# Max products in two pairs of PSUM banks, two exp banks in place of three: one core, attention with an MLP behind it

## The chip, the cores and the metric

One core of a Trainium2 chip runs the whole program. The metric is device time in microseconds, the median of several executions. TensorE (PE) multiplies matrices into PSUM, which has eight banks of 128 partitions x 512 fp32 here; VectorE (DVE) and ScalarE (ACT) read PSUM; GpSimd (POOL) works on SBUF alone; SyncE (SP) issues the DMAs.

## The reference, cut to what matters

```python
mod = (silu(c) @ w_mod).reshape(1, 6, 1, 512)          # sa, ca, ga, sb, cb, gb
h = layernorm(x) * (1 + ca) + sa                       # x: 2048 x 512
q = (h @ wq).reshape(2048, 32, 16); k = h @ wk; v = h @ wv   # 32 heads, one k and v of 16
p = softmax(einsum("hqd,kd->hqk", q, k) / 4)
x = x + ga * (einsum("hqk,kd->qhd", p, v).reshape(2048, 512) @ wo)
h = layernorm(x) * (1 + cb) + sb
x = x + gb * (gelu(h @ w1 + b1) @ w2 + b2)             # w1: 512 x 1376
```

All heads share one k and one v. Everything is fp32 in and out; products that need the precision are made from a high and a low part of each operand (three products in place of one).

## The kernel before, in words

**Units.** The 2048 queries are cut into eight blocks of 256, the 32 heads into eight groups of four: 64 units. The transposed queries of a unit lie in a tile `qst`, the keys in `ks`. Both have two row halves (s = 0: partitions 0 to 63, s = 1: 64 to 127), so that two products with 64 rows each can run side by side in TensorE's array, one per half. The functions take s as an argument.

**Two passes over the scores.** Softmax needs the largest score of each query. `Max.step` (L502) makes one *max product* (L509: 128 queries of one head against 512 keys, one PSUM bank `m`), and VectorE takes the maxima of its rows (L514, 128x512 to 128x1). A unit has 32 of them, the program 2048. When a unit is complete, `put_max` (L530) takes the last maxima, transposes them and sends them by DMA into extra rows of `qst`, from where they take part in the second pass. `sexp` (L576) makes one *exp product* (L589: 128 keys against 512 queries, bank `e0`, `e1` or `e2`, or `x`), already less the maximum, and ScalarE writes its exponential to SBUF (L590). There are 2048 of these too. `pv` (L592) multiplies the exponentials with v: 16 products of L601 per block, which use all 128 rows, into bank `v`.

**PSUM before.** Three banks for maxima (tag `m`), three for exps (`e0`, `e1`, `e2`), one for accumulation (`v`), one (`x`) for everything else: late q projections, the output projection, the MLP. Where no such job holds `x`, the plain half cycles put their last max product there.

**The order is written by hand.** All five engines run their instructions in the order in which the Python code issues them; a counter `clock` stands for time, and `later(n, fn)` puts a step n ticks ahead. The main loop goes over the 64 units and, in each, over pairs of key steps X = K and Y = K + 1. One turn of it makes eight exp products and, by the leads of `lead`, usually eight max products (for units some six half cycles ahead), in two *half cycles*, each closed by a P.V block (`end_step`, L1295).

- If a *batch* is at hand (`take`: up to six products with 512 columns, or twelve with 256, of another job: w1, w2, the output projection `wops`, late q projections, transposes), each of its products is split by rows: `half(one, 0)` runs in the first half cycle, `half(one, 1)` in the second. These *fills* occupy one row half; the four max products and three exps are placed on the other, alternately, and the fourth exp follows the fills. Exp banks are 0, 1, 2, 0.
- Without a batch (`plain`, L1323), two exps and two max products go to each row half.

`issue` (L1275) merges the lists of the two row halves into one order for TensorE: every entry has a length, and the list whose lengths add up to less is served next. A fill has 0.75 of its length, so that fills are issued a little early.

**What else shares the engines.** VectorE also drains w1's results and the output projection, ScalarE does Square and Tanh of GELU, POOL the rest of GELU and all splitting in the main loop. The last block has no attention beside it (`fast`): its projection and MLP run alone at the end, and take their PSUM banks from a list `spread`.

Of the kernel before, what the change touches and what calls it, by code (L numbers as in the profile page):

```python
# [14 lines left out]
P = 128  # L15
# [33 lines left out]
def adaln_mqa_mlp(  # L49
# [70 lines left out]
    turns = [0]  # L120

    def ebank():
        turns[0] += 1
        return dict(tag=f"e{turns[0] % 3}", bufs=1)
# [145 lines left out]
    def keep_warm(n):  # L270

        for _ in range(n):
            ps = psum.tile([P, BQ], F32, name=f"idle{len(idles)}", tag="m", bufs=3)
            nc.tensor.matmul(ps, wkH[:, 0, :], wkH.rearrange("p k n -> p (k n)"), start=True, stop=True)
            idles.append(ps)
# [84 lines left out]
    def turn1(b, d):  # L360
        ps = psum.tile([P, BQ], F32, name=f"tp{b}_{d}", **ebank())
# [36 lines left out]
    def v_out(b):  # L398
        vt = vts.pop(b)
        pv_ = psum.tile([P, QT, 32], F32, name=f"vps{b}", **ebank())  # L400
# [83 lines left out]
    class Max:  # L484


        def __init__(self):
# [9 lines left out]
            self.mx, self.left, self.done = {}, list(size), 0  # L497
# [4 lines left out]
        def step(self, s, hold=None, **place):  # L502
            u, j, t, kc = self.todo[s].pop(0)
            T = blocks[units[u][0]][1] // P
            if u not in self.mx:
                self.mx[u] = att.tile([P, 4 * T, NKC], F32, name=f"mx{u}", tag="mx", bufs=2)
            m = psum.tile([P, 512], F32, name=f"m{u}_{j}_{t}_{kc}_{s}", **(place or dict(tag="m", bufs=3)))
            rows = slice(64 * s, 64 * s + 64)
            nc.tensor.matmul(m, qsts[u][rows, j, t * P:(t + 1) * P], ks[rows, kc * 512:(kc + 1) * 512],  # L509
                             start=True, stop=True)  # L510
            i = (s * 2 + j) * T + t

            def reduce():
                nc.vector.tensor_reduce(out=self.mx[u][:, i, kc:kc + 1], in_=m, axis=AX.X, op=ALU.max)  # L514
                self.left[u] -= 1
                if self.left[u] == size[u] // 2 and u > 1 and u + 1 < NU:
                    load_q(u + 1)
                if self.left[u] == 0:
                    put_max(u, self.mx.pop(u))

            self.done += 1
            if hold is None:
                reduce()
            else:
                hold.append(reduce)
# [4 lines left out]
    def put_max(u, mx):  # L530
# [31 lines left out]
        def reduce():  # L562
            nc.vector.tensor_reduce(out=mm[:, :4 * T], in_=mx, axis=AX.X, op=ALU.max)
# [123 lines left out]
    def rest(b, fast):  # L687
# [3 lines left out]
        spread = ["m", "e", "m", "e", "m", "e", "v"] if fast else ["x"]  # L691
        turn = [0]

        def bank():
            turn[0] += 1
            tag = spread[turn[0] % len(spread)]
            return ebank() if tag == "e" else dict(tag=tag, bufs=3 if tag == "m" else 1)
# [54 lines left out]
        return rest_steps(b, fast, rp, bank, ons, ready)  # L752
# [27 lines left out]
    def rest_steps(b, fast, rp, bank, ons, ready):  # L780
# [4 lines left out]
        for hf in range(w // HQ):  # L785
# [44 lines left out]
            for t in range(2):  # L830
                ps = psum.tile([P, D], F32, name=f"wops{b}_{hf}_{t}", **bank())
# [49 lines left out]
            if fast:  # L881
                tps = [psum.tile([P, 2, HQ], F32, name=f"tp2_{b}_{hf}_{dp}", **bank()) for dp in range(KD // 2)]
# [9 lines left out]
            else:  # L892
                for dp in range(KD // 2):
                    ps = psum.tile([P, 2, HQ], F32, name=f"tp2_{b}_{hf}_{dp}", **bank())
# [43 lines left out]
            if fast:  # L938
                group = {f: psum.tile([P, HQ], F32, name=f"w1ps{b}_{hf}_{f}", **bank()) for f in range(GROUP)}
# [9 lines left out]
            for f in range(GROUP if fast else 0, NF):  # L949
# [3 lines left out]
                ps = psum.tile([P, HQ], F32, name=f"w1ps{b}_{hf}_{f}", **bank())  # L953
# [22 lines left out]
            for t in range(2):  # L976
                sl = slice(t * P, (t + 1) * P)
                for cols in (slice(0, D), ):
                    place = dict(tag="m", bufs=3) if b == len(blocks) - 2 and t else bank()
                    ps = psum.tile([P, D], F32, name=f"w2ps{b}_{hf}_{t}_{cols.start}", **place)  # L980
# [156 lines left out]
    def chunk(n):  # L1137
        for _ in range(n):
            mp.step(mp.done % 2)
# [93 lines left out]
    def last_h(t):  # L1233
        if t == QT - 1:
# [10 lines left out]
            "wq 1": one(prep_wq, 1), "wq 2": one(prep_wq, 2), "wq 3": one(prep_wq, 3)}  # L1245
    for n, *names in SLOTS:
# [22 lines left out]
    while mp.done < lead[0]:  # L1269
        chunk(1)  # L1270
# [14 lines left out]
    def mixture(a, b):  # L1285

        out = []
        while a or b:
            if a:
                out.append(a.pop(0))  # L1290
            if b:
                out.append(b.pop(0))
        return out

# [9 lines left out]
    for u in range(NU):  # L1304
        for K in range(0, steps[u], 2):
            goal = lead[u] + (lead[u + 1] - lead[u]) * (K + 2) / steps[u]
            goal = min(goal, first[u + QBUFS] if u + QBUFS < NU else first[NU])
            n = max(0, 2 * round((goal - mp.done) / 2))

            def maxes(s, n, first_=1.0, held=None):  # L1310
                return [(1.0 if i else first_, lambda i=i: mp.step(s, held if i == 2 else None)) if mp.has(s) else (0.0, lambda: None)
                        for i in range(n)]

            def exps(s, which):
                return [(1.0, lambda K=K, j=j, bank=bank: sexp(u, K, j, s, bank)) for K, j, bank in which]
# [114 lines left out]
```

## Time and profile before

| | |
|---|---|
| three runs, median | 1601.61 us (1600.05 to 1605.82) |
| profiled execution | 1599.49 us |
| its span, first to last instruction | 1597.6 us |
| mean granted TensorE clock | 0.996 |
| maxima L514 on VectorE | 2048, 1271.4 us busy |
| exponentials L590 on ScalarE | 2048, 1069.4 us busy |
| first P.V block after the span's start | 83.4 us |

A group of the profile names the line, the engine, the operation and the tiles (`mx<-m`: tile mx is written, tile m is read). PE rows are products, PEld rows the loading of their stationary operand; a product of one row half appears as 64 rows. A wait is written as engine and line that waited, then what it waited for. In the timeline, neighbouring instructions of one group are merged, with their count behind an x.

### The profile page before, as it was taken

How to read it: one execution, taken by the hardware profiler on the slowest of the kernel's cores; microseconds unless marked ns; L12 is line 12 of the kernel's file. 1: busy time of each engine (PE TensorE's matmuls, PEld its weight loads, DVE VectorE, ACT ScalarE, POOL GpSimd, SP SyncE). 2: the span in 40 equal slices, each digit the busy share in tenths (PEclk: the TensorE clock that was granted, in tenths of full speed). 3: DMA queues.
4: the chain of work that ended last, by engine and by line, in shares of the span. 5: the costliest groups of instructions: out<-in, count | busy, mean ns of one | idle time of the engine just before them, and what ended most of it. 6: DMA issues, size and time to landing. Idle time of an engine off the chain costs nothing.

```text
span 1597.6 us, 41064 instructions
## 1 busy us (share of the span) xinstructions
PE 1560.3 (98%) x16369; PEld 1006.3 (63%) x16369; DVE 1412.9 (88%) x2473; ACT 1203.0 (75%) x2393; POOL 666.1 (42%) x1176
## 2 busy tenths in 40 slices
PE   5999999999999999999999999999999999999998
PEld 3466665557665676657665676656666576656667
DVE  6899999899999998999989999999999999999715
ACT  5577778778777887778877887778877787778853
POOL 4445344747422571246413462234602474225711
PEclk8999999999999999999999999999999999999999
DMA  7136312313022220303112120213112130122232
GB/s 257 73 109 205 117 68 71 125 32 107 17 63 65 68 68 25 103 17 106 32 44 84 53 85 22 78 42 98 42 35 91 42 98 18 62 72 64 80 132 74
DMA packets 79285, 121.59 MB, mean 76 GB/s; under 512 B 15774, under 2 KB 52382, under 8 KB 78836
## 3 DMA queue, kind: packets, MB, share of 16 engines
q1 hardware_dynamic: 79076, 118.95, 23.2%
q8 instruction: 128, 2.10, 0.6%
q14 instruction: 65, 0.53, 0.1%
q10 hardware_dynamic: 16, 0.00, 0.0%
HBM read 91.13 MB, written 27.27 MB: 74 GB/s over the span
## 4 chain that ended last, share of the span: by engine, by line
PE 90%; DVE 6%; DMA 2%; POOL 1%; SPq 1%; ACT 0%; issue 0%; DVEq 0%; POOLq 0%
PE acc L601 30%; PE m L509 22%; PE e L589 17%; PE w1ps L184 8%; DVE mx L514 5%; PE w2ps L184 4%; PE wops L184 2%; PE qps L184 1%; PE w2ps L178 1%; DMA xt<-in_A_x_dram 1%; PE w1ps L178 1%; PE tp L184 1%; PE kps L160 1%; DMA qst<-dq 1%; DVE st L807 0%; DMA os<-drs 0%
## 5 line engine op out<-in xcount | busy, mean ns | idle before, releaser
L514 DVE TENSOR_REDUCE mx<-m 128x1 f32<-128x512 f32 x2048 | 1271.4, 682 | 107.6 <-PE m L509 81.3
L590 ACT ACTIVATE p<-e 128x512 f32<-128x512 f32 x2048 | 1069.4, 599 | 311.1 <-PE e L589 233.2
L509 PE MATMUL m<-ks,qst 64*128 64x512 f32 x2048 | 823.9, 425 | 17.4 <-DVE mx L514 11.0
L589 PE MATMUL e<-qst,ks 64*128 64x512 f32 x2048 | 739.1, 409 | 2.8 <-ACT p L590 1.5
L601 PE MATMUL acc<-p,va 128*32 128x256 f32 x8192 | 550.5, 386 | 0.6 <-DMA qst<-dq 0.6
L509 PEld LDWEIGHTS m<-ks,qst 64*128 64x128 f32 x2048 | 364.1, 184 | 185.8 <-DVE mx L514 157.0
L589 PEld LDWEIGHTS e<-qst,ks 64*128 64x128 f32 x2048 | 366.6, 185 | 85.2 <-ACT p L590 59.5
L601 PEld LDWEIGHTS acc<-p,va 128*32 128x32 f32 x8192 | 214.9, 109 | 220.6 <-issue 115.7
L184 PE MATMUL w1ps<-h2H,w1t 64*128 64x256 f32 x1232 | 236.3, 288 | 0.0
L558 POOL TENSOR_SCALAR mt<-turned 8x32 f32<-8x32 f32 x256 | 53.2, 208 | 362.4 <-DVE turned L564 350.4
L184 PEld LDWEIGHTS w1ps<-h2H,w1t 64*128 64x128 f32 x1232 | 184.2, 185 | 31.7 <-issue 23.0
L184 PE MATMUL w1ps<-h2L,w1t 64*128 64x256 f32 x616 | 169.4, 275 | 0.0
L184 PE MATMUL w2ps<-w2H,gH 64*128 64x512 f32 x286 | 118.1, 413 | 0.0
L184 PE MATMUL w2ps<-w2L,gH 64*128 64x512 f32 x286 | 117.4, 411 | 0.0
L184 PE MATMUL w2ps<-w2H,gL 64*128 64x512 f32 x286 | 117.4, 410 | 0.0
L184 PEld LDWEIGHTS w1ps<-h2L,w1t 64*128 64x128 f32 x616 | 113.8, 185 | 0.0
L920 POOL TENSOR_SCALAR tt<-tt 128x256 f32<-128x256 f32 x77 | 31.1, 404 | 162.8 <-ACT tt L919 162.8
L744 POOL TENSOR_TENSOR os<-os 128x256 f32<-128x256 f32 x28 | 20.6, 734 | 100.9 <-DMA os<-drs 100.2
L921 POOL TENSOR_TENSOR tt<-tt,z 128x256 f32<-128x256 f32 x77 | 57.1, 741 | 6.4
L135 POOL TENSOR_TENSOR gL<-z,gH 128x256 fp32r<-128x256 f32 x77 | 56.8, 738 | 6.4
L931 POOL TENSOR_TENSOR z<-tt,z 128x256 f32<-128x256 f32 x77 | 56.5, 733 | 6.0
L930 POOL TENSOR_TENSOR tt<-tt,z 128x256 f32<-128x256 f32 x77 | 56.7, 736 | 0.0
(188 smaller groups left out, 1498.2 us busy)
## 6 DMA issues: line engine op xcount, KB each, us to landing
w1t<-dw SPq DMA_DIRECT2D x82, 512.0 KB
qst<-dq SPq DMA_DIRECT2D x128, 64.0 KB
do<-oc SPq DMA_DIRECT2D x64, 128.0 KB
dw<-w1s SPq DMA_DIRECT2D x11, 512.0 KB
xt<-in_A_x_dram SPq DMA_DIRECT2D x4, 1024.0 KB
dq<-qH SPq DMA_DIRECT2D x16, 256.0 KB
dq<-qL SPq DMA_DIRECT2D x16, 256.0 KB
qst<-dq SPq DMA_DIRECT2D x128, 32.0 KB
```

The costliest lines, as they stand in the source:

```text
L135: eng_l.tensor_tensor(out=dst_l, in0=src, in1=raw(dst_h), op=ALU.subtract)
L178: nc.tensor.matmul(ps, a, b_, start=first_, stop=last_)
L184: nc.tensor.matmul(ps, a[rows], b_[rows], start=first_ and s == 0, stop=last_ and s == 1)
L509: nc.tensor.matmul(m, qsts[u][rows, j, t * P:(t + 1) * P], ks[rows, kc * 512:(kc + 1) * 512], start=True, stop=True)
L514: nc.vector.tensor_reduce(out=self.mx[u][:, i, kc:kc + 1], in_=m, axis=AX.X, op=ALU.max)
L558: nc.gpsimd.tensor_scalar(out=mt[:, g:g + 32], in0=turned[g:g + 4 * T, :], scalar1=1.0, scalar2=0.0, op0=ALU.mult, op1=ALU.add)
L589: nc.tensor.matmul(e, ks[rows, kt * P:(kt + 1) * P], rhs, start=True, stop=True)
L590: nc.scalar.activation(ptiles[u, K][:, j, s, :], e, AF.Exp, scale=0.25)
L601: ins = nc.tensor.matmul(accs[u][32 * cidx:32 * cidx + 32, :], va[:, kt, :], rhs, start=kt == 0, stop=kt == NKT - 1)
L921: nc.gpsimd.tensor_tensor(out=tt, in0=tt, in1=z, op=ALU.mult)
L930: nc.gpsimd.tensor_tensor(out=tt, in0=tt, in1=z, op=ALU.mult)
L931: nc.gpsimd.tensor_tensor(out=z, in0=tt, in1=z, op=ALU.add)
```

## The change

It replaces the three `m` banks and one `e` bank by two tiles of two banks each (`pairs`). A pair gets two max products of the same row half in the main loop, of both row halves at the start (`both`); VectorE takes the maxima of both in one instruction, whose output is two columns of `mx`. The number of products is the same. Exps have banks `e0` and `e1`, and `x` in plain half cycles where no job holds it.

The half cycles are ordered anew: in one with a batch the fills' row half begins with an exp, and the other has two max products, an exp, a max product, an exp, a max product, an exp. Plain half cycles have one pair on each row half. The results of the last block and of the start go to `single` banks of the pairs where they went to `m`.

```diff
+    pairs = [psum.tile([P, 2, 512], F32, name=f"m{i}") for i in "ab"]
+    singles = [pair[:, i, :] for pair in pairs for i in range(2)]
+    turns = {"e": 0, "m": 0, "both": 3}
...
+    def eplace(shape, name):
+        turns["e"] += 1
+        i = turns["e"] % turns["both"]
+        if i == 2:
+            return shaped(singles[3], shape)
+        return psum.tile(shape, F32, name=name, tag=f"e{i}", bufs=1)
...
-        def step(self, s, hold=None, **place):
+        def product(self, out, s):
...
-            nc.tensor.matmul(m, qsts[u][rows, j, t * P:(t + 1) * P], ks[rows, kc * 512:(kc + 1) * 512],
+            nc.tensor.matmul(out, qsts[u][rows, j, t * P:(t + 1) * P], ks[rows, kc * 512:(kc + 1) * 512],
                              start=True, stop=True)
...
-                nc.vector.tensor_reduce(out=self.mx[u][:, i, kc:kc + 1], in_=m, axis=AX.X, op=ALU.max)
...
+        def reduce(self, pair, one, two):
+            u, i = one
+            assert two[0] == u and two[1] > i
+            nc.vector.tensor_reduce(out=self.mx[u][:, i:two[1] + 1:two[1] - i], in_=pair, axis=AX.X, op=ALU.max)
+            self.left[u] -= 2
...
+        def both(self):
+
+            pair = self.next_pair()
+            self.reduce(pair, *[self.product(pair[:, s, :], s) for s in range(2)])
+
+        def pair(self, s, hold=None):
...
+            return [(1.0, lambda: ends.append(self.product(pair[:, 0, :], s))), (1.0, last)]
...
-        spread = ["m", "e", "m", "e", "m", "e", "v"] if fast else ["x"]
+        spread = ["m", "e", "m", "e", "m", "m", "v"] if fast else ["x"]
...
     def chunk(n):
-        for _ in range(n):
-            mp.step(mp.done % 2)
+        for _ in range(n // 2):
+            mp.both()
...
+    turns["both"] = 2
     for n, *names in SLOTS:
...
-            n = max(0, 2 * round((goal - mp.done) / 2))
+            n = max(0, round((goal - mp.done) / 4))
...
-            def plain(s, K, t, n, banks):
-
-                a, b_, c_, d = banks
-                one = mixture(exps(s, [(K, 0, a), (K, 1, c_)]), maxes(s, n))
-                other = maxes(t, n)
+            def beside(batch, s, exps, go_on_=None, held=None):
+
+                fills = halves(batch, s) + ([(0.0, go_on_)] if go_on_ else [])
+                ms = [m for i in range(n) for m in mp.pair(1 - s, held if i == 1 else None)]
+                issue([(1.01, exps[0][1])] + fills, ms[:2] + [exps[1]] + ms[2:3] + [exps[2]] + ms[3:] + [exps[3]])
+
+            def plain(K, banks, more):
 
                 soon = any(planned and time <= clock[0] + 2 for time, _, planned in queue)
-                if not holder and not soon and mp.has(t) and n > 1:
-                    other[-1] = 1.0, lambda: mp.step(t, tag="x", bufs=1)
-                issue(one, exps(t, [(K, 0, b_)]) + other + exps(t, [(K, 1, d)]))
+                free = not holder and not soon
+                a, b_, c_, d = more if free else banks
+                one, other = mp.pair(1) if n > 1 else [], mp.pair(0) if n else []
+                issue([(1.01, exp(0, K, 0, a)[1])] + other + [exp(0, K, 1, d)], one + [exp(1, K, 0, b_), exp(1, K, 1, c_)])
...
             if batch:
-                groups = [mixture(maxes(1, n // 2, 0.0), exps(1, [(X, 0, 0), (X, 1, 1), (Y, 0, 2)])),
-                          halves(batch, 0) + exps(0, [(X, 0, 0)])]
-                issue(*(reversed(groups) if batch[0][3] else groups))
+                beside(batch, 0, [exp(0, X, 0, 0), exp(1, X, 0, 1), exp(1, X, 1, 0), exp(1, Y, 0, 1)])
             else:
-                plain(1, X, 0, (n + 2) // 4, (1, 2, 0, 1))
+                plain(X, (0, 1, 0, 1), (0, 1, "x", 0))
...
-                issue(mixture(maxes(0, n // 2, 0.0, reduces), exps(0, [(X, 1, 0), (Y, 0, 1), (Y, 1, 2)])),
-                      halves(batch, 1) + [(0.0, go_on_)] + exps(1, [(Y, 1, 0)]))
+                beside(batch, 1, [exp(1, Y, 1, 1), exp(0, X, 1, 0), exp(0, Y, 0, 1), exp(0, Y, 1, 0)], go_on_, reduces)
                 advance()
             else:
-                plain(1, Y, 0, n // 4, (2, 0, 1, 2))
+                plain(Y, (0, 1, 0, 1), (1, "x", 0, 1))
```

More of the change, by code (lines that the diff above doesn't have):

```diff
@@ new lines, in product, with next_pair @@
+            return u, ((s * 2 + j) * T + t) * NKC + kc
+        def reduce(self, pair, one, two):
[3 more added lines that the diff above has]
+            self.left[u] -= 2
+            if self.left[u] == size[u] // 2 and u > 1 and u + 1 < NU:
+                load_q(u + 1)
+            if self.left[u] == 0:
+                put_max(u, self.mx.pop(u))
+        def next_pair(self):
+            self.turn = 1 - self.turn
+            return pairs[self.turn]
@@ L751, in rest @@
         later(*((4, lambda: norm(0)) if fast else (2, fetch)))
-        return rest_steps(b, fast, rp, bank, ons, ready)
+        return rest_steps(b, fast, rp, place, ons, ready)
     early = {}
@@ L938, in rest_steps @@
             if fast:
-                group = {f: psum.tile([P, HQ], F32, name=f"w1ps{b}_{hf}_{f}", **bank()) for f in range(GROUP)}
+                group = {f: place([P, HQ], f"w1ps{b}_{hf}_{f}") for f in range(GROUP)}
                 for k in range(KD):
@@ L978, in rest_steps @@
                 for cols in (slice(0, D), ):
[L979 to L980 removed]
+                    ps = single([P, D]) if b == len(blocks) - 2 and t else place([P, D], f"w2ps{b}_{hf}_{t}")
                     ops = [(gH[:, f, sl], gL[:, f, sl], w2H[:, f, cols], w2L[:, f, cols]) for f in range(NF)]
@@ L1283, in issue @@
             at[g] += length
[L1285 to L1293, printed above, removed]
     def end_step(u, K):
@@ L1307, in adaln_mqa_mlp, with exp @@
             goal = min(goal, first[u + QBUFS] if u + QBUFS < NU else first[NU])
-            n = max(0, 2 * round((goal - mp.done) / 2))
[L1310 to L1315, printed above, removed]
+            n = max(0, round((goal - mp.done) / 4))
+            def exp(s, K, j, bank):
+                return 1.0, lambda: sexp(u, K, j, s, bank)
             def halves(batch, s):
```

62 lines of the change are left out of this document (32 added, 30 removed).

## Prediction

> **What bounds the kernel now.** I read the page's busy times first, then its chain and groups, then the waits, and last the timeline, half cycle by half cycle.
>
> ```profile
> PE 1560.3 (98%) x16369; PEld 1006.3 (63%) x16369; DVE 1412.9 (88%) x2473; ACT 1203.0 (75%) x2393; POOL 666.1 (42%) x1176
> PE 90%; DVE 6%; DMA 2%; POOL 1%; SPq 1%; ACT 0%; issue 0%; DVEq 0%; POOLq 0%
> L514 DVE TENSOR_REDUCE mx<-m 128x1 f32<-128x512 f32 x2048 | 1271.4, 682 | 107.6 <-PE m L509 81.3
> L590 ACT ACTIVATE p<-e 128x512 f32<-128x512 f32 x2048 | 1069.4, 599 | 311.1 <-PE e L589 233.2
> ```
>
> VectorE is busy 88% of the span, nearly all of it with the maxima that the change merges, so it looks like a bound. The chain says otherwise: TensorE carries 90% of it, VectorE 6%. An average over the span cannot settle that, so I went to the stage. A half cycle runs from one P.V block (16 products of line 601) to the next. Here is one with a batch of w1 products, first block to next (lines left out are w1 products and weight loads):
>
> ```profile
> 713.89 1.07 PE L601 MATMUL acc<-p,va 128*32 128x256 f32 x16
> ...
> 714.89 0.38 PE L184 MATMUL w1ps<-h2H,w1t 64*128 64x256 f32 x1
> ...
> 714.90 0.49 PE L509 MATMUL m<-ks,qst 64*128 64x512 f32 x1
> ...
> 715.23 0.39 PE L589 MATMUL e<-qst,ks 64*128 64x512 f32 x1
> ...
> 715.46 0.39 PE L509 MATMUL m<-ks,qst 64*128 64x512 f32 x1
> ...
> 715.66 2.06 ACT L590 ACTIVATE p<-e 128x512 f32<-128x512 f32 x4 [1.03 <-PE e L589]
> 715.70 0.39 PE L589 MATMUL e<-qst,ks 64*128 64x512 f32 x1
> ...
> 716.31 0.18 PEld L589 LDWEIGHTS e<-qst,ks 64*128 64x128 f32 x1
> ...
> 716.38 0.42 PE L589 MATMUL e<-qst,ks 64*128 64x512 f32 x1
> 716.40 0.41 PE L509 MATMUL m<-ks,qst 64*128 64x512 f32 x1
> ...
> 716.74 1.07 PE L601 MATMUL acc<-p,va 128*32 128x256 f32 x16
> ```
>
> The P.V block holds TensorE 1.00 us (713.89 to 714.89). Then each row half of the array streams seven products: maxima and exps alternate on one, 0.233 us apart (715.23, 715.46, 715.70); fills and one exp run on the other. The last starts at 716.40, 1.50 after the first, and 0.34 later the next block begins: 2.85 us in all, and TensorE never stands. So in such a half TensorE is the bound, and VectorE (four maxima by 0.62, which is 1271.4 / 2048, or 2.48 us) fits under it. One thing is already at the edge: the fourth exp uses the first one's bank. ScalarE takes the first exp at 715.66, for 0.60 us; its weight load comes at 716.31, 0.05 after the end, and the product starts at 716.38, just when its turn has come.
>
> How many halves are like this follows from the groups of fill products:
>
> ```profile
> L184 PE MATMUL w1ps<-h2H,w1t 64*128 64x256 f32 x1232 | 236.3, 288 | 0.0
> L184 PE MATMUL w1ps<-h2L,w1t 64*128 64x256 f32 x616 | 169.4, 275 | 0.0
> L184 PE MATMUL w2ps<-w2H,gH 64*128 64x512 f32 x286 | 118.1, 413 | 0.0
> L184 PE MATMUL wops<-woH,onH 64*128 64x512 f32 x112 | 49.7, 443 | 0.3 <-DVE mx L514 0.3
> L184 PE MATMUL tp<-ident,xh 64*128 64x128 f32 x224 | 33.5, 288 | 0.0
> L601 PE MATMUL acc<-p,va 128*32 128x256 f32 x8192 | 550.5, 386 | 0.6 <-DMA qst<-dq 0.6
> ```
>
> w1: 1848 at 12 a half, 154. w2: 3 x 286 half products are 429 whole ones, 13 outputs of 33, each in six batches that take two halves: 156. wops: 3 x 112 at 6, 56. tp: 224 at 8, 28. The late q projections: 14 of two batches by the code, 56. That is 450 of the 512 halves (8192 / 16); about 60 have no fills. By the timeline 14 of the 450, at the end, have no maxima left, so 436 are of the kind shown.
>
> **The change part by part.**
>
> *Pairs of maxima on VectorE.* 2048 instructions of 512 elements become 1024 of 1024. No row has one of 1024. A small reduction bounds what an instruction costs beside its elements:
>
> ```profile
> L563 DVE TENSOR_REDUCE mm<-mx 128x8 f32<-128x32 f32 x64 | 11.2, 175 | 0.2
> ```
>
> From 32 to 512 elements the mean goes from 175 to 682 ns, 1.06 ns an element, so a pair takes about 682 + 541 = 1223 ns, and back to back 621 + 541 = 1162; at worst two old ones, 1364. I take 1.16: VectorE loses 1024 x (1.242 - 1.162), about 80 us of work, between 0 and 90. In 436 halves that is slack on an engine that is not last, and brings nothing. The Trainium skill ("Perfetto Trace Analysis", Optimizing Scalar/DVE Operations) puts the per-instruction overhead of VectorE on PSUM at about 125 ns and says that grouping helps if the engine is saturated; by its figure 128 us of VectorE work would go, an estimate. The condition is what fails here: the half above is full on TensorE.
>
> *Two exp banks.* This is the expensive part. In a half with fills the new order has exps at places 0, 2, 4 and 6 of the seven, in banks 0, 1, 0, 1 (the second half 1, 0, 1, 0). So the third exp waits until ScalarE has read the first, and the fourth for the second. The price of one such return has a row already: a half without fills that starts with an exp and whose last exp reuses its bank.
>
> ```profile
> 259.17 0.50 PE L589 MATMUL e<-qst,ks 64*128 64x512 f32 x2
> ...
> 259.50 0.62 PE L509 MATMUL m<-ks,qst 64*128 64x512 f32 x3
> ...
> 259.71 2.07 ACT L590 ACTIVATE p<-e 128x512 f32<-128x512 f32 x4 [0.56 <-PE e L589]
> ...
> 260.36 0.18 PEld L589 LDWEIGHTS e<-qst,ks 64*128 64x128 f32 x1 [0.32 <-ACT p L590]
> 260.36 0.50 PE L589 MATMUL e<-qst,ks 64*128 64x512 f32 x1
> 260.78 0.59 PEld L601 LDWEIGHTS acc<-p,va 128*32 128x32 f32 x16 [0.24 <-issue]
> 260.79 1.07 PE L601 MATMUL acc<-p,va 128*32 128x256 f32 x16
> ```
>
> Start 259.17; ScalarE begins 0.54 later, needs 0.60 (L590's mean 599), and 0.05 after it the weights load: 1.19 us from the start. The product streams from 1.29 (a load on an idle array costs 0.10 more: 0.33 to the next product, not 0.233). In the new half the third exp's turn would be 1.03. Behind it on TensorE's queue stand two fills, a max product and the fourth exp; on its row half two places follow, 0.233 each, so the fourth exp starts at 1.29 + 0.47 = 1.76. Its own bank agrees: second exp at place 2, 0.56; ScalarE takes it behind the first, at 0.54 + 0.49 = 1.03, until 1.63; free at 1.68. Block 0.34 later, at 2.10, plus 1.00 for P.V: 3.10 us against 2.855. **436 x 0.245 = 107 us.** ScalarE's other work (1203.0 - 1069.4 = 134 us) lies between the fourth exp's end (about 2.8) and the next first exp (3.10 + 0.54), a gap of 0.8 per half that the present halves have as well (2.06 of 2.85 us used); I charge nothing. Bounds: +0.15 a half if the restart after a wait costs less than 0.10 and the places close up (65 us); half of those 134 us on the path as well (+67 us) at the top.
>
> *The 14 halves without maxima.* The queue there is exp, exp, then the third exp, then the fills, so all fills stand behind the wait. Today:
>
> ```profile
> 1510.61 1.07 PE L601 MATMUL acc<-p,va 128*32 128x256 f32 x16
> ...
> 1513.25 1.07 PE L601 MATMUL acc<-p,va 128*32 128x256 f32 x16
> ```
>
> 2.64 with five fills; with six, 0.2 more. New: fills start at 1.29, six end at 1.29 + 5 x 0.233 + 0.34 = 2.80, plus 1.00; about one us more than today. 14 x 0.95 = 13 us.
>
> *Halves without fills.* Where bank x is free (some 32 by the timeline) three banks rotate, the last exp reuses the first one's, and the half stays at the 2.62 of the fence. Where x is taken (28) today's half is held by VectorE:
>
> ```profile
> 710.95 1.07 PE L601 MATMUL acc<-p,va 128*32 128x256 f32 x16
> ...
> 713.46 0.18 PEld L509 LDWEIGHTS m<-ks,qst 64*128 64x128 f32 x1 [0.97 <-DVE mx L514]
> ```
>
> From 710.95 to 713.89 it lasts 2.94. The pair removes that wait, but the fourth exp, now in bank 1, is late next: free at 1.68, block 0.43 later, 3.11. 28 x 0.17 = 5 us.
>
> *The start and the end.* Some 28 pairs are made before the first exp; 0.08 each is 2 us if VectorE leads there:
>
> ```profile
> 60.00:83.40 23.40, 21.77 (x103) 9.66 (x104) 20.58 (x35) 10.53 (x24) 7.55 (x17) 0.96 0.16 51
> 1543.00:1597.00 54.00, 49.97 (x306) 41.10 (x304) 27.37 (x68) 16.50 (x42) 5.34 (x6) 1.00 0.29 108
> ```
>
> VectorE has 20.58 of 23.40 us, so I credit 2, and bound it by 5 either way, since transposes there lose the third bank. At the end TensorE has 50 of 54 us, and the other placing of results changes none of its products: nothing. The held maxima, the loads of qst and the sends of the row maxima are issued by the same counts; the six-half lead hides them.
>
> **Sum**: 107 + 13 + 5 - 2 = +123 on the profiled execution's 1599.5 us (span 1597.6), which lies 2 under the median of the runs shown: **1722 us**.
>
> **The rivals.** *The waits are covered, and only the locked halves move* (faster): if an exp bank came back within four places, 4 x 0.233 = 0.93 us of the half's start, the exps would be on time, the 28 halves would go from 2.94 to 2.62, 9 us, and the start gives 2: 1588. The point is 0.93; the fence above shows 1.19, against it. Chance 0.05.
>
> Two rows of the waits bear on the others:
>
> ```profile
> PEld m L509 <- DVE mx L514: 157.0, 368, 1.1
> ...
> PEld e L589 <- ACT p L590: 59.5, 210, 0.6
> ```
>
> *VectorE is the bound after all* (faster): all of the 80 us come off, 1520. For it: 88% busy and 157 us of weight loads put down to it; against it: the 2.85 that TensorE fills, under which such a load waits unseen. Chance 0.03. The Trainium skill's grouping rule, named above, would make it 1472 by its figure.
>
> *Nothing measurable*: waits and gains cancel, 1600. Chance 0.03.
>
> *ScalarE's other work falls into the shortened ring* (slower still): its tanh, square and copies delay the first exp, and with two banks every delay reaches TensorE. For it: the 59.5 us of today may be so few only because a third bank absorbs such delays. All 134 us on the path give 1856, half of them 1789. Chance 0.11. My forecast has the remaining 0.78.
>
> **How the numbers follow.** The forecast's own bounds run from 1722 - 42 - 10 = 1670 to 1789, the first with 65 in place of 107 and the small terms at their best. A little is added below for the cases between it and the rivals: 1660 to 1785. A measurement of this kernel can tell 0.5%, 8 us, from no change. Slower: 0.78 + 0.11 = 0.89. Same 0.03. Faster 0.05 + 0.03 = 0.08.
>
> **What would show it.** Right: P.V blocks about 3.10 us apart in halves with fills, two idle gaps of TensorE per half put down to the exp line of ScalarE, that wait rising from 59.5 us to over 150, VectorE near 1330 us busy with pairs of 1.2 us, waits on the maxima nearly gone. Wrong: blocks still 2.85 apart, or the third exp's load less than 1.1 us after the half's start, or maxima still the last wait.

## The result, and the profile after

The changed kernel takes 1730.62 us (median of four runs, 1729.12 to 1732.84) against 1601.04 for the kernel before beside it: ratio 1.0804, 95% interval 1.0779 to 1.0829. It is slower by 129.6 us; the forecast was 123 slower. The profiled execution's span grew from 1597.6 to 1728.2 us, +130.6, at the same granted clock of 0.996.

The page after (line numbers have moved: exp products are L623, exponentials L624, max products L522, maxima L530, P.V L635), its busy times, its chain and its groups:

```profile
PE 1678.1 (97%) x16369; PEld 999.2 (58%) x16369; DVE 1379.2 (80%) x1449; ACT 1248.1 (72%) x2393; POOL 668.1 (39%) x1176
...
PE 89%; ACT 3%; DVE 3%; DMA 1%; POOL 1%; issue 1%; SPq 1%; ACTq 0%; POOLq 0%; DVEq 0%
...
L624 ACT ACTIVATE p<-e 128x512 f32<-128x512 f32 x2048 | 1113.9, 596 | 375.3 <-PE e L623 326.6
...
L530 DVE TENSOR_REDUCE mx<-ma 128x2 f32<-128x1024 f32 x512 | 626.5, 1224 | 244.2 <-PE ma L522 236.9
L530 DVE TENSOR_REDUCE mx<-mb 128x2 f32<-128x1024 f32 x512 | 625.2, 1221 | 5.4 <-PE mb L522 5.0
```

TensorE's busy time rose from 1560.3 to 1678.1 us for the same 16369 products: they overlap less, and the busy share (97%) does not show the loss. The chain hides it too: it gives TensorE 90% before and 89% after. What changed is who waits. The waits after, with total, number and longest in us:

```profile
PEld e L623 <- ACT p L624: 358.8, 1108, 1.1
ACT p L624 <- PE e L623: 326.6, 459, 1.5
DVE mx L530 <- PE ma L522: 236.9, 425, 1.4
```

The first was 59.5 us in 210 waits. VectorE now waits for its pairs, where TensorE used to wait for VectorE: the waits of the max products' weight loads for VectorE, 157.0 us before, come to 21 us. The exp products wait for ScalarE, ScalarE waits for exp products: a ring of two banks.

A half cycle with w1 products, the kind that the prediction worked out, from the timeline after (left out: fills, weight loads, POOL):

```profile
776.12 1.07 PE L635 MATMUL acc<-p,va 128*32 128x256 f32 x16
...
777.12 0.50 PE L623 MATMUL e<-qst,ks 64*128 64x512 f32 x1
...
777.12 0.50 PE L522 MATMUL ma<-ks,qst 64*128 64x512 f32 x1
...
777.65 2.27 ACT L624 ACTIVATE p<-e 128x512 f32<-128x512 f32 x4 [0.53 <-PE e L623]
...
777.70 0.39 PE L623 MATMUL e<-qst,ks 64*128 64x512 f32 x1
...
778.30 0.18 PEld L623 LDWEIGHTS e<-qst,ks 64*128 64x128 f32 x1
778.31 0.50 PE L623 MATMUL e<-qst,ks 64*128 64x512 f32 x1
...
778.65 0.40 PE L522 MATMUL mb<-ks,qst 64*128 64x512 f32 x1
...
778.79 0.18 PEld L623 LDWEIGHTS e<-qst,ks 64*128 64x128 f32 x1
778.89 0.40 PE L623 MATMUL e<-qst,ks 64*128 64x512 f32 x1
...
779.22 1.07 PE L635 MATMUL acc<-p,va 128*32 128x256 f32 x16
```

Count from 777.12. ScalarE starts 0.53 later; the third exp's weights load at 1.18 (bank 0 is back); behind it a max product at 1.53 and the fourth exp at 1.77, whose weights loaded at 1.67. The next P.V block starts at 2.10, which is 3.10 after the first. The half shown is no exception: in 413 of the 436 halves with fills and maxima the third exp's weights load at 1.18 or 1.19 and the fourth's at 1.67 or 1.68.

The starts of all P.V blocks, sorted by what lies between them, put the whole difference in place. (In the 60 halves without fills, `x` is free in 32, called free below, and taken in 28, called locked.)

| stretch | number | before, us | after, us | difference | forecast |
|---|---|---|---|---|---|
| halves with fills and maxima | 436 | 1253.2 | 1356.9 | +103.7 | +107 |
| halves with fills, no maxima | 14 | 38.5 | 53.4 | +14.9 | +13 |
| halves without fills | 60 | 168.4 | 179.1 | +10.7 | +5 |
| up to the first P.V block | | 83.4 | 83.6 | +0.2 | -2 |
| from the last P.V block on | | 54.1 | 55.2 | +1.1 | 0 |
| sum | | 1597.6 | 1728.2 | +130.6 | +123 |

Two stretches of TensorE show the smaller terms. A half without maxima:

```profile
1631.15 1.07 PE L635 MATMUL acc<-p,va 128*32 128x256 f32 x16
1632.15 0.50 PE L623 MATMUL e<-qst,ks 64*128 64x512 f32 x2
1633.33 0.49 PE L623 MATMUL e<-qst,ks 64*128 64x512 f32 x1 [0.68 <-ACT p L624]
1633.33 0.50 PE L198 MATMUL w2ps<-w2H,gH 64*128 64x512 f32 x1
1633.82 0.50 PE L623 MATMUL e<-qst,ks 64*128 64x512 f32 x1
1633.82 0.49 PE L198 MATMUL w2ps<-w2H,gL 64*128 64x512 f32 x1
...
1634.94 1.07 PE L635 MATMUL acc<-p,va 128*32 128x256 f32 x16
```

All fills stand behind the third exp (1633.33, 1.18 after 1632.15), as forecast. But the second fill is held too: the fourth exp, ahead of it on the queue, waits for its own bank until 1633.82. So this half, with five fills, is 3.79 us. The halves with six last no longer (3.79 to 3.80), because there two fills are issued ahead of the fourth exp and use its wait; the forecast had let the fills run on at 0.233 in both.

The locked half, forecast at 3.11, comes in three lengths: 14 of the 28 at 3.10, seven at 3.65, seven at 3.76. One of the last kind, with the engine that made it late:

```profile
753.59 1.07 PE L635 MATMUL acc<-p,va 128*32 128x256 f32 x16
753.70 1.02 ACT L903 ACTIVATE h<-tp,sb,cb 128x256 f32<-128x256 f32 x2
...
754.60 0.60 ACT L624 ACTIVATE p<-e 128x512 f32<-128x512 f32 x1
...
755.26 0.18 PEld L623 LDWEIGHTS e<-qst,ks 64*128 64x128 f32 x1 [1.07 <-ACT p L624]
...
756.03 1.23 DVE L530 TENSOR_REDUCE mx<-ma 128x2 f32<-128x1024 f32 x1 [1.36 <-PE ma L522]
...
757.17 1.22 DVE L530 TENSOR_REDUCE mx<-mb 128x2 f32<-128x1024 f32 x1
```

ScalarE does two activations of the MLP's input (L903) ahead of the previous half's last exponential (754.60). That exponential frees bank 0, with which the new half begins: its first exp loads at 755.26, where 754.59 was due, 0.67 late. The 3.65 halves follow the free ones, in which VectorE falls behind; there the second pair's first product waits for VectorE:

```profile
736.46 0.18 PEld L522 LDWEIGHTS mb<-ks,qst 64*128 64x128 f32 x1 [0.70 <-DVE mx L530]
...
737.67 0.18 PEld L623 LDWEIGHTS e<-qst,ks 64*128 64x128 f32 x1 [0.85 <-ACT p L624]
```

Some exps stand behind that product on TensorE's queue; the bank return of 1.2 us then starts from 736.46, and the last exp loads at 737.67.

### The profile page after: what moved, and what is told of

Same layout as the page of the kernel before. It is cut to its first block, busy times and chain, and to the rows that moved or that the text cites. A ratio compares the mean times of both kernels' runs of the same rounds, so it can differ in the third digit from the quotient of the medians.

```text
span 1728.2 us, 39835 instructions
## 1 busy us (share of the span) xinstructions
PE 1678.1 (97%) x16369; PEld 999.2 (58%) x16369; DVE 1379.2 (80%) x1449; ACT 1248.1 (72%) x2393; POOL 668.1 (39%) x1176
## 4 chain that ended last, share of the span: by engine, by line
PE 89%; ACT 3%; DVE 3%; DMA 1%; POOL 1%; issue 1%; SPq 1%; ACTq 0%; POOLq 0%; DVEq 0%
PE e L623 29%; PE acc L635 27%; PE mb L522 8%; PE w1ps L198 7%; PE w2ps L198 6%; PE qps L198 2%; DVE mx L530 2%; PE ma L522 2%; PE wops L198 2%; ACT p L624 2%; PE tp L198 1%; PE kps L174 1%; PE mb L192 1%; PE ma L192 1%; PE w2ps L192 0%
## 5 line engine op out<-in xcount | busy, mean ns | idle before, releaser
L624 ACT ACTIVATE p<-e 128x512 f32<-128x512 f32 x2048 | 1113.9, 596 | 375.3 <-PE e L623 326.6
L623 PE MATMUL e<-qst,ks 64*128 64x512 f32 x2048 | 908.3, 452 | 22.9 <-ACT p L624 21.7
L530 DVE TENSOR_REDUCE mx<-ma 128x2 f32<-128x1024 f32 x512 | 626.5, 1224 | 244.2 <-PE ma L522 236.9
L530 DVE TENSOR_REDUCE mx<-mb 128x2 f32<-128x1024 f32 x512 | 625.2, 1221 | 5.4 <-PE mb L522 5.0
L623 PEld LDWEIGHTS e<-qst,ks 64*128 64x128 f32 x2048 | 370.9, 184 | 398.4 <-ACT p L624 358.8
L635 PE MATMUL acc<-p,va 128*32 128x256 f32 x8192 | 548.9, 385 | 0.0
L522 PE MATMUL mb<-ks,qst 64*128 64x512 f32 x1024 | 393.4, 401 | 2.0 <-DVE mx L530 1.9
L522 PE MATMUL ma<-ks,qst 64*128 64x512 f32 x1024 | 372.2, 447 | 6.3 <-DMA qst<-dq 5.1
L635 PEld LDWEIGHTS acc<-p,va 128*32 128x32 f32 x8192 | 214.1, 109 | 214.2 <-issue 110.2
L198 PE MATMUL w1ps<-h2H,w1t 64*128 64x256 f32 x1232 | 226.9, 277 | 0.0
L522 PEld LDWEIGHTS mb<-ks,qst 64*128 64x128 f32 x1024 | 184.5, 186 | 26.8 <-DVE mx L530 19.4
L198 PEld LDWEIGHTS w1ps<-h2H,w1t 64*128 64x128 f32 x1232 | 196.6, 185 | 5.7
L522 PEld LDWEIGHTS ma<-ks,qst 64*128 64x128 f32 x1024 | 149.9, 185 | 11.5 <-DVE ve L210 5.3
```

The source lines that it names most:

```text
L198: nc.tensor.matmul(ps, a[rows], b_[rows], start=first_ and s == 0, stop=last_ and s == 1)
L522: nc.tensor.matmul(out, qsts[u][rows, j, t * P:(t + 1) * P], ks[rows, kc * 512:(kc + 1) * 512], start=True, stop=True)
L530: nc.vector.tensor_reduce(out=self.mx[u][:, i:two[1] + 1:two[1] - i], in_=pair, axis=AX.X, op=ALU.max)
L623: nc.tensor.matmul(e, ks[rows, kt * P:(kt + 1) * P], rhs, start=True, stop=True)
L624: nc.scalar.activation(ptiles[u, K][:, j, s, :], e, AF.Exp, scale=0.25)
L635: ins = nc.tensor.matmul(accs[u][32 * cidx:32 * cidx + 32, :], va[:, kt, :], rhs, start=kt == 0, stop=kt == NKT - 1)
```

## The experiments

The theory: the third exp bank is the loss, by the return of a bank (1.19 us after the half's start) against the place where the bank is needed again. Rivals: the new order of products, the instruction over two banks, or VectorE. All ratios are to the kernel before.

**Two exp banks in the old order.** Only the bank numbers of the kernel before are changed; single maxima in three banks as before (one bank idle).

```diff
-        return dict(tag=f"e{turns[0] % 3}", bufs=1)
+        return dict(tag=f"e{turns[0] % 2}", bufs=1)
...
-                groups = [mixture(maxes(1, n // 2, 0.0), exps(1, [(X, 0, 0), (X, 1, 1), (Y, 0, 2)])),
-                          halves(batch, 0) + exps(0, [(X, 0, 0)])]
+                groups = [mixture(maxes(1, n // 2, 0.0), exps(1, [(X, 0, 0), (X, 1, 1), (Y, 0, 0)])),
+                          halves(batch, 0) + exps(0, [(X, 0, 1)])]
...
```

> The kernel before with its order and its single maxima, but two exp banks instead of three (one bank left unused). Theory (the return of an exp bank by ScalarE): in a half with fills the first exp stands at place 1, ScalarE has it from 0.77 to 1.37 us, the third exp loads at 1.42, the fourth waits for the second until 1.91, next P.V block at 2.34: half 3.34 against 2.855, 436 x 0.485 = 211; halves without fills about 3.11, +18; the 14 without maxima +8: about 1837 us, slower than the change itself. Rival (the new order or the pairs cost the time, the number of exp banks does not): 1600 to 1610.

1833.5 us, ratio 1.1465 (1.1448 to 1.1482). Halves with fills and maxima last 3.33 us. Its timeline:

```profile
801.63 1.07 PE L601 MATMUL acc<-p,va 128*32 128x256 f32 x16
...
802.64 0.50 PE L509 MATMUL m<-ks,qst 64*128 64x512 f32 x1
...
802.98 0.39 PE L589 MATMUL e<-qst,ks 64*128 64x512 f32 x1
...
804.06 0.18 PEld L589 LDWEIGHTS e<-qst,ks 64*128 64x128 f32 x1 [0.43 <-ACT p L590]
...
804.55 0.18 PEld L589 LDWEIGHTS e<-qst,ks 64*128 64x128 f32 x1 [0.30 <-ACT p L590]
...
804.97 1.07 PE L601 MATMUL acc<-p,va 128*32 128x256 f32 x16
```

The old order begins with a max product, so the first exp streams at 0.34, and its bank is back at 1.42 instead of 1.18. The missing bank costs 0.48 us a half in the old order; the new order, which begins with an exp, wins 0.23 of it back. So the reordering is no cause of the loss: it halves it. This run changes nothing but the number of exp banks, so it shows the cause by itself.

**Half of the exponentials, half of the maxima.** Two kernels made from the changed one. In the first, ScalarE makes the exponentials of 256 of the 512 columns and P.V uses these twice (half of the exponentials are left out). In the second, VectorE takes the maxima of 256 of each 512 keys (half of the maxima's input is left out, and the exponent has a smaller factor).

```diff
-        nc.scalar.activation(ptiles[u, K][:, j, s, :], e, AF.Exp, scale=0.25)
+        nc.scalar.activation(ptiles[u, K][:, j, s, 0:256], e[:, 0:256], AF.Exp, scale=0.25)
...
```
```diff
-            nc.vector.tensor_reduce(out=self.mx[u][:, i:two[1] + 1:two[1] - i], in_=pair, axis=AX.X, op=ALU.max)
+            nc.vector.tensor_reduce(out=self.mx[u][:, i:two[1] + 1:two[1] - i], in_=pair[:, :, 0:256], axis=AX.X, op=ALU.max)
...
```

> The changed kernel, but ScalarE takes the exponentials of only 256 of the 512 columns of each exp product, and the P.V products read these 256 for both heads: half of the exponentials are left out. Theory (bank return): one exponential falls from 0.60 to about 0.38 us, so the third exp loads at 0.97 where its turn is 0.95, the fourth at 1.43 where its turn is 1.42: halves with fills back to about 2.87; the 14 without maxima stay about 0.85 longer than before: 1600 to 1625 us. Rival (pairs, order or VectorE cost the time): within 1 per cent of the change, 1715 to 1731.

> The changed kernel, but VectorE takes the maxima over only 256 of the 512 keys of each max product, about 0.7 us a pair in place of 1.22, with the exponent scaled down so that it stays finite: half of the maxima are left out. Theory (bank return): halves with fills stay at 3.10, only halves without fills where a pair comes late gain (7 of 3.65 us): 1720 to 1730 us. Rival (a pair of 1.22 us holds TensorE longer than two singles did): below 1680.

Half of the exponentials: 1625.84 us, ratio 1.0156 (1.0135 to 1.0177), 1 us above the range; most halves with fills and maxima last 2.86 to 2.88 us. Half of the maxima: 1723.77, ratio 1.0785 (1.0765 to 1.0805); such halves still 3.10. A group of each:

```profile
L624 ACT ACTIVATE p<-e 128x256 f32<-128x256 f32 x2048 | 774.1, 384 | 577.5 <-PE e L623 451.8 <-PE w2ps L198 1.9 <-PE mb L522 1.7
```
```profile
L530 DVE TENSOR_REDUCE mx<-ma 128x2 f32<-128x512 f32 x512 | 354.2, 692 | 545.4 <-PE ma L522 538.1 <-PE w1ps L198 7.2
```

Exponentials 0.21 us shorter take 105 us off; pairs of maxima 0.53 us shorter take 7. The 28 us that the first kernel's profiled span still lies over the kernel before are mostly in the halves with fills and maxima (15; 67 of them last over 2.95, against 14 before) and in those without maxima (10). The waits of exp products in the second kernel are 364.5 us, no fewer than the 358.8 of the changed one. The loss is ScalarE's hold on two banks: shorter exponentials alone could also mean that ScalarE is short of time, but the run with two banks in the old order has the same exponentials as the kernel before and differs from it in the banks alone. What the maxima do matter for is the seven halves of 3.65, which went to 3.10; the seven of 3.76 stayed, as they should if ScalarE's L903 makes them.

**Pairs of banks, but each product reduced by itself.** The banks and the order of the changed kernel, 2048 maxima instructions as before.

```diff
+            for k, (u, i) in enumerate((one, two)):
+                nc.vector.tensor_reduce(out=self.mx[u][:, i:i + 1], in_=pair[:, k, :], axis=AX.X, op=ALU.max)
+                self.left[u] -= 1
```

> The changed kernel with the same four banks, order and exp banks, but VectorE takes the maxima of each product in an instruction of its own, as before. Theory (return of the exp banks): pairing is worth nothing where TensorE and ScalarE set the pace; halves with fills stay at 3.10, the total within 6 us of 1730. Rival (pairing itself costs, since the first product of a pair waits for the second): 1700 or less. Rival (pairing already saves time that the exp banks cost again): 1750 or more.

1734.67 us (1731.11 to 1736.37), ratio 1.0838 (1.0819 to 1.0857); halves with fills and maxima 3.10 again. The two groups of maxima are 659.2 + 655.0 = 1314.2 us busy against 1251.7 with pairs. Those 62 us of VectorE show as 4 us between the medians, and the runs of the two kernels overlap; in the profiled executions only the halves without fills are longer, 181.4 us in all against 179.1.

**The exps of a half moved apart.** The changed kernel with the second exp first on its row half and the third behind all four max products, so that more lies between two uses of a bank.

```diff
-                issue([(1.01, exps[0][1])] + fills, ms[:2] + [exps[1]] + ms[2:3] + [exps[2]] + ms[3:] + [exps[3]])
+                issue([(1.01, exps[0][1])] + fills, [exps[1]] + ms + exps[2:])
```

> The changed kernel with another order in halves with fills: an exp first on each row half, then the four max products, then the other two exps, so that the third exp comes to its place only after its bank is free. Theory (bank return): with two banks and four exps in a half no order helps: the second exponential runs from 1.03 to 1.63 us, the fourth exp loads at 1.68 and the P.V block follows at 2.11: halves of 3.11, 1730 us within 8. Rival (the order with exps at places 2 and 4 costs the time): 1650 or less.

1730.94 us, ratio 1.082 (1.080 to 1.084): the same. In its timeline:

```profile
777.24 0.50 PE L623 MATMUL e<-qst,ks 64*128 64x512 f32 x2
777.77 1.09 ACT L624 ACTIVATE p<-e 128x512 f32<-128x512 f32 x2 [0.43 <-PE e L623]
...
778.51 0.40 PE L623 MATMUL e<-qst,ks 64*128 64x512 f32 x1
...
778.91 0.50 PE L623 MATMUL e<-qst,ks 64*128 64x512 f32 x1
...
779.34 1.07 PE L635 MATMUL acc<-p,va 128*32 128x256 f32 x16
```

The third exp no longer holds anything up (1.27), and the fourth still comes at 1.67, since ScalarE ends the second exponential at 778.86, 1.62 after the half's start, and 0.05 later its bank is loaded for. So with two banks 1.67 + 0.43 + 1.00 = 3.10 is a floor for every order that keeps the four exps of a half between two P.V blocks: the first two can stream no earlier than the half's start. An order that puts a P.V block between the exps of a half was not run.

**Two repairs with two banks.** Without maxima, the fills go ahead of the waiting exps; halves without fills begin with the other bank, so that the late exponential is not the one they need first.

```diff
+                if not n:
+                    exps = [exp(*o, (s + i) % 2) for i, o in enumerate(exps[1:] + exps[:1])]
+                    issue(exps[:3], fills + exps[3:])
+                    return
...
-                plain(X, (0, 1, 0, 1), (0, 1, "x", 0))
+                plain(X, (1, 0, 1, 0), (1, 0, "x", 1))
...
-                plain(Y, (0, 1, 0, 1), (1, "x", 0, 1))
+                plain(Y, (1, 0, 1, 0), (0, "x", 1, 0))
```

> The changed kernel with two repairs outside the main term. In the 14 halves without maxima the fills are issued as in the kernel before, ahead of the exps' waits: 3.80 to 3.90 should become 3.31 as with two exp banks in the old order, 7 us less. Halves without fills start with the bank that was not used last, so that the seven which follow the transposes (3.76) no longer wait for an exponential that stands behind two other activations on ScalarE: about 3.15, 4 us less. Together 1719, between 1715 and 1724. If the waits there have another cause, no change: 1730.

1719.54 us, ratio 1.075 (1.0733 to 1.0767). Halves without maxima fell from 3.80 to 3.31 (w2) and from 3.91 to 3.33 (w1), the 3.76 ones to 3.27 (3.15 expected), the 3.65 ones stayed at 3.62. Both readings of the small terms hold; together they are 11 us of the 130.

**Three exp banks in the new order.** The new order with single maxima in three banks and exps in banks 0, 1, 2, 0; fills first where there are no maxima.

```diff
+        return psum.tile(shape, F32, name=f"s{turns['m']}", tag="m", bufs=3)
...
+        i = turns["e"] % 3
...
+                exps = [exp(*o, bank % 3) for bank, o in enumerate(exps)]
+                issue([(1.01, exps[0][1])] + fills, ms[:2] + [exps[1]] + ms[2:3] + [exps[2]] + ms[3:] + [exps[3]])
...
+                plain(X, (0, 1, 2, 0), (0, 1, 2, 0))
...
```

> The changed kernel's order of half cycles, but single maxima in three banks and three exp banks (0, 1, 2, 0 in every half); in halves without maxima the fills go first as before. Theory (bank return): no exp waits past its place, halves with fills back at 2.855; the 28 halves without fills and without x go from 2.94 or 3.28 to about 2.65: 1590 us, between 1583 and 1605. Rival (the order costs): about 1725.

A miss: 1671.63 us, ratio 1.0452 (1.0436 to 1.0467), most halves with fills and maxima at 2.97, most without fills at 3.02. Its timeline:

```profile
800.77 0.49 PE L518 MATMUL m<-ks,qst 64*128 64x512 f32 x1
...
801.33 1.29 DVE L524 TENSOR_REDUCE mx<-m 128x1 f32<-128x512 f32 x2 [0.48 <-PE m L518]
...
802.07 0.18 PEld L518 LDWEIGHTS m<-ks,qst 64*128 64x128 f32 x1
...
802.41 0.39 PE L612 MATMUL e<-qst,ks 64*128 64x512 f32 x1
...
802.73 1.07 PE L624 MATMUL acc<-p,va 128*32 128x256 f32 x16
```

The fourth max product reuses the bank of the first, which VectorE holds from 801.33 for 0.68: it loads at 802.07, 1.30 after 800.77. With two max products at the start, the new order brings this turn forward, and the last exp stands behind it. The wait has moved from ScalarE's banks to VectorE's. That I had not counted: as it stands, the new order needs four banks for maxima, and eight banks do not give four and three beside `v` and `x`.

**The same with half of the maxima** tests that reading: VectorE gives each bank back 0.26 us sooner (again 256 of 512 keys, and a smaller exponent).

```diff
-            nc.vector.tensor_reduce(out=self.mx[u][:, i:i + 1], in_=out, axis=AX.X, op=ALU.max)
+            nc.vector.tensor_reduce(out=self.mx[u][:, i:i + 1], in_=out[:, 0:256], axis=AX.X, op=ALU.max)
```

> The kernel with the new order, single maxima in three banks and three exp banks, which came out at 1671.6 us and not at 1590; now VectorE takes the maxima over 256 of the 512 keys, with the exponent scaled down so that it stays finite: half of the maxima are left out. New theory (the fourth max product, at place 5 in the new order, waits for the bank of the first, which VectorE reads from 0.56 to 1.24 us): the bank is free at about 1.0, before its turn at 1.19, so halves with fills fall from 2.97 to 2.86, those without from 3.02 to about 2.62: 1671 - 50 - 24 = 1597 us, 1588 to 1606. Rival (the new order itself costs 0.12 a half): 1640 or more.

1582.9 us, ratio 0.9899 (0.9882 to 0.9915): the wait was VectorE's. The fourth max product's weights now load 1.04 to 1.14 after the half's start. The time is below the range I gave: most halves with fills last 2.81 to 2.84, under the 2.85 that I had called full on TensorE, while most halves without fills last 2.75, not the 2.62 expected.

**Can the full work have it?** The last exp is issued ahead of the last max product, only that one's result is held, and halves without fills use `x` for it.

```diff
-                issue([(1.01, exps[0][1])] + fills, ms[:2] + [exps[1]] + ms[2:3] + [exps[2]] + ms[3:] + [exps[3]])
+                issue([(1.01, exps[0][1])] + fills, ms[:2] + [exps[1]] + ms[2:3] + [(1.45, exps[2][1]), exps[3]] + ms[3:])
...
```

> A version after what the runs so far say: three exp banks and three max banks with single maxima, the new order of halves with fills, but with its last exp ahead of its last max product, so that this product comes to its place (load at 1.42) after VectorE has left the first one's bank (1.30), and the fourth exp at place 5 (load at 1.19) just as its bank comes free (1.19); halves without fills as in the kernel before, a max product first on one row half. Theory (every half runs at TensorE's pace if no bank is asked for before its return): halves with fills 2.82 to 2.84 as in the run with half maxima, 436 x 0.03 = 13 us under the kernel before, and 4 us in the halves without fills: 1582 us, 1574 to 1592, ratio 0.99. Rival (the short halves of that run came from the shorter VectorE instructions, or a late fill holds the exp that is issued behind it): 1597 or more.

A miss: 1614.11 us, ratio 1.0091 (1.0077 to 1.0105). Most halves with w2 products are at 2.84 to 2.85, most with w1 at 2.90 to 2.95, and 57 of all at 3.0 or more. So the new order with three exp banks comes near the old one, but, as far as tried, not past it once the maxima are whole. The rival's late fill is not shown to be the reason. In 35 of the 152 w1 halves the third exp does start late (1.12 after the start in one, and the fourth at 1.35). But in the other 117 the third is on time, mostly at 1.03 to 1.05, and still the last max product starts only at 1.58 or later, about when the last fill does, against 1.52 in w2 halves.

**The old kernel, its locked halves mended.** Three exp banks and three max banks as before; only the halves without fills begin with a max product on both row halves, and `x` takes the other list's last one.

```diff
-                if not holder and not soon and mp.has(t) and n > 1:
-                    other[-1] = 1.0, lambda: mp.step(t, tag="x", bufs=1)
-                issue(one, exps(t, [(K, 0, b_)]) + other + exps(t, [(K, 1, d)]))
+                if not holder and not soon and mp.has(s) and n > 1:
+                    one[-1] = 1.0, lambda: mp.step(s, tag="x", bufs=1)
+                issue(one, other[:1] + exps(t, [(K, 0, b_)]) + other[1:] + exps(t, [(K, 1, d)]))
```

> The kernel before; only in halves without fills one row half begins with a max product in place of an exp, and bank x goes to the last max product of the other row half. Theory (bank return): in the 28 such halves in which x is taken, the fourth max product waits for the first one's bank, which VectorE then frees 0.21 us earlier: 2.94 to about 2.73, 3.28 to about 3.0; the other 32 stay at 2.61. 6 us less: 1594, ratio 0.996 (0.993 to 1.000). Rival (VectorE's rate sets these halves): no change, 1600.

1595.3 us (12 runs) against 1599.05 (17), ratio 0.9973 (0.9964 to 0.9983): the best of all with the whole work. It is faster than both kernels, than the old one by 0.3%: the interval lies below 1, though the gain is under the 0.5% that the prediction called measurable. The halves without fills account for it, 164.4 us in all against 168.4, where 6 us had been forecast. A locked half:

```profile
711.83 1.07 PE L601 MATMUL acc<-p,va 128*32 128x256 f32 x16
...
714.14 0.18 PEld L509 LDWEIGHTS m<-ks,qst 64*128 64x128 f32 x1 [0.78 <-DVE mx L514]
...
714.57 1.07 PE L601 MATMUL acc<-p,va 128*32 128x256 f32 x16
```

The fourth max product loads 2.31 after the P.V block in place of 2.51, and the half lasts 2.74 in place of 2.94; of the 28, 14 came to that, seven to 2.85, and those of 3.3 to about 3.2. What the prediction credited to the pairs in these halves, the end of that wait, comes in part without them.

## Why the prediction was right

**The bound.** TensorE, not VectorE with its 88% busy, was the right reading: pairs or single maxima, whole or half, move the changed kernel by 4 to 7 us. The chain's 90% alone would not have carried it, as it is 89% after, where TensorE waits in every half; the half cycle read row by row did. No run takes VectorE's work alone out of the kernel before. The nearest, half of the maxima in the new order with three banks for each, lies 16 us under it, far from the 80 of the rival.

**Two exp banks.** The step carried the result. A bank's return was read from one row of before as 1.19 us and measured 1.18; fourth exp forecast at 1.76, measured 1.77; block at 2.10, measured 2.10; half 3.10, measured 3.10. The 0.10 us of the restart lie behind the third exp (1.19, then 1.53) and not ahead of it (1.29), which leaves the sum the same. The working gave the fourth exp two limits, its turn and its bank, and they fall together; the run with the exps moved apart, in which the third waits for nothing, is as long, so the bank alone is enough. The term of 107 us came to 103.7, because the old halves averaged 1253.2 / 436 = 2.874: about a quarter of them were longer than the 2.855 of the one shown. The experiments with two banks in the old order and with half of the exponentials show the cause.

**Halves without maxima.** 14.9 against 13. The place of the wait was right; the working ended it at the third exp and left out that the fourth holds the fills a second time. This touches only some of them: the six halves with six fills last the 3.80 worked out, while the six with five fills, for which the working gives 0.23 less, last as long, which is 1.4 us in all.

**Halves without fills.** 10.7 against 5. The free halves stayed (nearly all 2.60 to 2.63) and half of the locked ones came to the forecast 3.10. The old ones were misread by a little: seven of the 28 lasted 3.3, not 2.94, so 3.11 for all would have cost 2 us and not 5. The step that failed is "the fourth exp ... is late next": in seven halves VectorE, behind after free halves, was late before it (3.65), and in seven ScalarE's other work was (3.76).

**ScalarE's other work, charged at nothing.** Here the forecast was too kind by a little, and the rival held a grain of truth. Besides the 3.76 halves (7 x 0.66 = 5 us), some 22 halves last 3.28, 0.18 more than the rest, 4 us in all; one of them:

```profile
770.74 0.18 PEld L623 LDWEIGHTS e<-qst,ks 64*128 64x128 f32 x1 [0.41 <-ACT p L624]
...
770.88 0.37 ACT L645 COPY oc<-acc 128x256 f32<-128x256 f32 x1 [0.43 <-PE acc L635]
...
771.15 0.42 ACT L960 ACTIVATE tt<-tt 128x256 f32<-128x256 f32 x1
...
771.47 2.27 ACT L624 ACTIVATE p<-e 128x512 f32<-128x512 f32 x4
```

A copy and a tanh stand ahead of the first exponential, which starts 0.73 after the half's first exp (770.74), not 0.53; it is so in 21 of the 22. So about 9 of the 134 us lie on the path. The rival that put half or all of them there is out.

**VectorE's work.** The sign was right, the size wrong: the forecast was near 1330 us busy, it is 1379.2. The pair's mean of 1223 ns was met (1224 and 1221), but a pair seldom queues behind a pair, so the maxima's busy time is 1251.7 us, 1024 times the 1.22 of a pair by itself, and fell by 1271.4 - 1251.7 = 20 us, not 80. The miss cost nothing, as this engine is not last. Whether the start gained the 2 us credited for the same saving is not shown: it took 83.6 us after against 83.4 before, but 79.4 in the kernel with the exps moved apart, whose start is the same code.

**The other rivals.** That the waits are covered needed a return within 0.93 us; it is 1.18. That all cancels, or that VectorE is the bound, is refuted by the time and by the half maxima.

Left open: why halves with three exp banks and shortened maxima reach 2.82, under the 2.85 that the prediction read as TensorE's own limit, and why the last max product comes late in the w1 halves of the last try with three exp banks.

## What to carry to other kernels

Count the banks of each ring by its period: a bank is back one product, one wait and one eviction after its product starts (here 1.18 us), and the number of banks is that time over the spacing of the products that use them, rounded up, with the evicting engine's side work on top. The spacing within the half counts, not the mean: four exps in 2.85 us are 0.71 apart, by which two banks would do (1.18 / 0.71 = 1.7), but two places of the new order are 0.47, and 1.18 / 0.47 = 2.5 asks for three. A bank taken from the engine that feeds the bound costs on every turn, while the instruction saved on an engine with slack brings nothing. Before an order is changed, look where each ring's reuse falls in the new one, and what stands behind it on the same queue.

## What the runs showed of the hardware that was not expected

One instruction over two banks saves less than a busy time suggests. Here "queued" means that the products were ready before VectorE was. Queued, the pair at 756.03 above is followed by the next at 757.17: 1.14 us apart, though each shows 1.22 or 1.23. Single maxima of before, queued:

```profile
65.82 2.48 DVE L514 TENSOR_REDUCE mx<-m 128x1 f32<-128x512 f32 x4
```

The last of four lasts 0.68, so they start (2.48 - 0.68) / 3 = 0.60 apart, and a pair saves 2 x 0.60 - 1.14 = 0.06 us. The kernel with the pairs' products reduced singly agrees: (1314.2 - 1251.7) / 1024 = 0.06. The Trainium skill ("Perfetto Trace Analysis", Optimizing Scalar/DVE Operations) gives VectorE an overhead of about 125 ns per instruction on PSUM. A merge that spared one of these whole would save 0.125 us, an estimate; here about half of that was found, and the measurement decides.
